# Twelve products for the last two up blocks of a delta-rule and hard-swish kernel, with their buffers given back

## The chip, the cores and the metric

One core of a Trainium2 chip runs the whole program. The metric is device time in microseconds (us), the median of several executions. The engines are TensorE (PE in the profile; its weight loads are PEld), VectorE (DVE), ScalarE (ACT), GpSimd (POOL) and SyncE (SP), which issues most DMAs here. Each engine works through its own queue in order, and semaphores make one wait for another. Every number of type float32 stays float32; in the profile a matmul of such numbers appears as two passes, each with its weight load.

## The reference

The first half is a delta-rule attention over 4 batches, 8 heads, 768 tokens and 48 channels; its output, as 3072 rows of 384, goes through an MLP with a hard-swish of 2048 channels.

```python
def _attn_ref(q, k, v, beta):
    B, H, S, D = q.shape                       # 4, 8, 768, 48
    k_n = k / (np.linalg.norm(k, axis=-1, keepdims=True) + 1e-06)
    state = np.zeros((B, H, D, D), dtype=np.float32)
    y = np.zeros_like(q)
    for t in range(S):
        kt, vt, bt = (k_n[:, :, t], v[:, :, t], beta[:, :, t, None])
        y[:, :, t] = np.einsum('bhd,bhde->bhe', q[:, :, t], state)
        v_old = np.einsum('bhde,bhd->bhe', state, kt)
        state = state + bt[:, :, :, None] * np.einsum('bhd,bhe->bhde', kt, vt - v_old)
    return y

def _moe_ref(x, w_in, w_out):                  # x 3072 x 384, w_in 384 x 2048, w_out 2048 x 384
    h = x @ w_in
    relu6 = np.clip(h + 3.0, 0.0, 6.0)
    g = h * relu6 / 6.0
    return g @ w_out
```

## The kernel before

**Tiles.** The 768 tokens are cut into N = 24 chunks of C = 32; a chunk t covers the four batches, 128 rows in all, one on each partition. Two chunks make a block of 256 rows for the MLP, so there are 12 blocks, 0 to 11.

**The chain.** For each chunk, `prep` (L492) scales the keys (`kb`, on GpSimd), builds a mask times beta (`mb`, L473, GpSimd), turns keys and queries on TensorE (`pt`) and copies them with ScalarE into a tile KQ (L521), multiplies them (`sc`) and lets VectorE make L and LB of the product (L545). `scaled` (L481) makes `bkb`, the keys times beta, on GpSimd. A triangular system is solved for each chunk: chunk 0 by `product` (L556), chunks 1 to 4 by `halves_of` and `join` (L653), with a scratch tile VY, and later groups of four by `inverse` (L733), some 60 VectorE instructions between two transpositions (L456, L460). `chain` (L774) then runs the recurrence over the chunks: `ks` (keys and queries times state, L793), R (VectorE, L806), `pz` (L814), Z (ScalarE, L901, into R's tile), `su` and the state's update (L912, L928), `py`, y (L830, L806, L849), and the transposition `yt` (L859), which is copied into the MLP's input xT (L863).

**The MLP.** `up` (L956) makes a block's hidden rows in 16 steps f of 128 channels. A step is three products over NKT = 3 slices of 128 input channels, each a matmul with 128 x 128 weights and 256 columns, added up in one of NPM = 4 PSUM banks (`ph`, L968). ScalarE's relu (L976) and VectorE's minimum and product (L979) make the hard-swish g; the bank is free when L979 has read it. `up_by_eleven` (L1032) is used in its place for blocks 10 and 11 (UF = 10, L993). There, two steps f and two halves of the columns are joined to a 2 x 2 problem in quarters for the first two slices, done with seven products for eight, and the third slice is added with four plain ones: eleven products of 128 columns in place of twelve. It needs sums of weights (`weight_sums`, L1007, GpSimd, during the down product of block 9) and of inputs (`token_sums`, L1023, VectorE, L1029), and puts g together from the first four products with ScalarE's copy (L1053), GpSimd's sums (L1005), VectorE's sums (L1069, L1070) and ScalarE's and VectorE's last steps (L1076, L1080, L1083). The first four products of a pair are issued by `begin(j)`, the other seven by `end(j)`.

The down product of block 0 and 1 is plain (`down`, L1122). From block 2 on `down_by_seven` (L1176) works with quarters again: A11 and A12 are g of f = 0 to 7 for the first and the second 128 rows, A21 and A22 those of f = 8 to 15. Seven products of 192 columns (`po`, L1196) of eight f each follow in the order 1, 4, 2, 5, 7, 6, 3, each in two halves of four f; VectorE makes sums in the place of A22, A21, A11 and A12 (L1182) between them, ScalarE copies results (L1203), and VectorE joins them (L1206) into `o`, which goes to DRAM (L1120).

**The order.** Nothing is reordered by a scheduler. Up to chunk 5 the order is the text ORDER, in which each word advances one generator by a step: `v` is one DMA of V, `q`, `k` and `w` those of queries, keys and weights. From chunk LS = 5 on, a loop of NU = 15 units per chunk advances the chain by a plan and takes one unit of the MLP (a step f, or half a down product) and two or three steps of the inverse in each. Block 9's up product runs beside chunk 20's chain, block 10's beside chunk 22's, and block 11's after the last chain has ended.

**Buffers.** `sums_in` (L116) is the memory of the weight sums. Until they are made it serves as spare room: two VY tiles (NVY = 2), every second mask `mb` of the early chunks, and the first of eight `bkb`. KQ has NKQ = 6 tiles, LB has 7, V has NVF = 2; R has one, which Z uses as well, so that R of chunk t waits for `py` and `su` of t - 1 (L882). `ring` and `needs` only assert at build time that the order allows a reuse; the waits themselves come from the tiles.

Of the kernel before, what the change touches and what calls it, by code (L numbers as in the profile page):

```python
# [38 lines left out]
k*2 v h4 i2*2 u rb i2 gb n9 i2 u i2 v i2 ru i2 gu i2 u ru i2*3 q gu i2 c n9 u k i2 u i2 u ru gu q  # L39
ru i2 gu i2 k n9 i2 u h4 y4 i2*2 n9 u y4 i2 q u*2 i2 u n9 ru i2*3 q k gu q*2 i2 n9 q i2*3 n9 u k  # L40
n9 q e i2*4 ru u gu y4 h4 e n9 u y4 k n9 k*2 i2 k*5 i2*2 k*3 ru k ru gu i2 u gu p9 u e i2 u i2*5 e
u i2*4
# [4 lines left out]
def kernel(  # L47
# [61 lines left out]
    def first(g):  # L109
# [3 lines left out]
    LA, LE, LS = 6, 4, G0 + GS  # L113
    NKB, NQB, NBKB, NLB, NKQ, NVY = 2, 4, 8, 7, 6, 2
    NPR = NFC // 2
    sums_in = persist.tile([P, 3, NPR, P], FP32, name="sums_in")  # L116
    spares = sums_in[:].rearrange("p n j c -> p (n j c)")
    vys = [spares[:, 4 * H * C * i : 4 * H * C * (i + 1)] for i in range(NVY)]
    mb_spare = spares[:, 8 * H * C : 10 * H * C]
    bkb_spare = spares[:, 10 * H * C : 10 * H * C + H * DP].rearrange("p (h w) -> p h w", w=DP)  # L120
    assert 10 * H * C + H * DP == 3 * NPR * P
    kbufs = [persist.tile([P, H, DP], FP32, name=f"kb{i}") for i in range(NKB)]
    qbufs = [persist.tile([P, H, DP], FP32, name=f"qb{i}") for i in range(NQB)]
    bkbufs = [bkb_spare] + [
        persist.tile([P, H, DP], FP32, name=f"bkb{i}") for i in range(1, NBKB)
    ]

    def bkb_of(t):
        return bkbufs[t if t < NBKB else 1 + (t - 1) % (NBKB - 1)]

# [46 lines left out]
    NVF = 2  # L177
# [284 lines left out]
    def mask(t):  # L462
        early = t < LS + LE
        if t > 1 or not early:
            needs(("L", t - (2 if early else 1)))
        if early and t % 2 == 0:
            mb = mb_spare.rearrange("p (e a j w) -> p e a j w", e=2, j=2, w=C)
        else:
            mb = work.tile([P, 2, NP, 2, C], FP32, name="mb", bufs=1)
        mbs[t] = mb  # L470
        needs("beta")
        for e in range(2):
            nc.gpsimd.tensor_tensor(  # L473
                out=mb[:, e],
                in0=beta_tok[:, t, e:H:2].unsqueeze(2).unsqueeze(3).to_broadcast([P, NP, 2, C]),
                in1=mask2[:].unsqueeze(1).to_broadcast([P, NP, 2, C]),
                op=ALU.mult,
            )
        yield

    def scaled(t):  # L481
        needs(("kb", t), *pad(t), *([("bkb", t - NKB)] if t >= NKB else []))
        if t >= NBKB:
            needs(("su", t - NBKB + 1))
        nc.gpsimd.tensor_tensor(
            out=bkb_of(t)[:, :, 0:D], in0=kbufs[t % NKB][:, :, 0:D],
            in1=beta_tok[:, t, 0:H].unsqueeze(2).to_broadcast([P, H, D]), op=ALU.mult,
        )
        past.add(("bkb", t))
        yield  # L490
# [65 lines left out]
    def product(t):  # L556
# [10 lines left out]
        ring("VY", NVY, ("x", t))  # L567
        VYTF = vys[t % NVY].rearrange("p (n w) -> p n w", w=H * C)
# [84 lines left out]
    def join(t):  # L653
# [7 lines left out]
        ring("VY", NVY, ("x", t))  # L661
        tiles = vys[t % NVY].rearrange("p (n h c) -> p n h c", n=4, c=C)
# [111 lines left out]
    def chain(t, whole=True):  # L774
# [8 lines left out]
        bkb = bkb_of(t)  # L783
# [96 lines left out]
        else:  # L880
            needs("parity")
            needs(("BZ", t - 1), ("su", t - 1))  # L882
# [17 lines left out]
        Zt = Rt if t > 0 else work.tile([P, DM], FP32, name="R", bufs=1)  # L900
# [21 lines left out]
        past.add(("su", t))  # L922
# [18 lines left out]
    mode = {"slow": False}  # L941
# [50 lines left out]

    UF = 10  # L993
    S1, S2, S4 = (sums_in[:, i] for i in range(3))

    def w_tiles(s, i):
        return w_in[:, s].rearrange("p (j i c) -> p j i c", i=2, c=P)[:, :, i]

    W11, W12, W21, W22 = w_tiles(0, 0), w_tiles(1, 0), w_tiles(0, 1), w_tiles(1, 1)
    W13, W23 = w_tiles(2, 0), w_tiles(2, 1)  # L1000
    T1x, T2x, T4x = (beta_tok[:, 8 * i : 8 * i + 8, 8:24] for i in range(3))
    assert H == 8 and N == 24

    def plus_minus(out, a, b, op):
        nc.gpsimd.tensor_tensor(out=out, in0=a, in1=b, op=op)  # L1005

    def weight_sums():  # L1007
        for j in range(0, NPR, 2):
            r = slice(j, j + 2)
            plus_minus(S1[:, r], W21[:, r], W22[:, r], ALU.add)  # L1010
            yield
            plus_minus(S2[:, r], S1[:, r], W11[:, r], ALU.subtract)
            yield
            plus_minus(S4[:, r], W12[:, r], S2[:, r], ALU.subtract)
            yield
            plus_minus(W21[:, r], W11[:, r], W21[:, r], ALU.subtract)
            yield

    def x_tiles(blk):
        x = xTs[blk]  # L1020
        return [x[:, s, i * P : i * P + P] for s in range(NKT) for i in range(CB)]

    def token_sums(blk):  # L1023
        needs(("seam", blk * CB), ("seam", blk * CB + 1), ("up", blk - 1))
        B11, B12, B21, B22, _, _ = (
            x.rearrange("p (a b) -> p a b", b=16) for x in x_tiles(blk)
        )
        for out, a, b in ((T1x, B12, B11), (T2x, B22, T1x), (B12, B22, B12), (T4x, B21, T2x)):
            nc.vector.tensor_tensor(out=out, in0=a, in1=b, op=ALU.subtract)  # L1029
        past.add(("sums", blk))  # L1030

    def up_by_eleven(blk):  # L1032
        needs(("sums", blk))
        mode["slow"] = True
        B11, T3x, B21, B22, B31, B32 = x_tiles(blk)
        phs, ready = {}, {}

        def mm(ph, n, w, x, start=False, stop=False):
            nc.tensor.matmul(  # L1039
                ph[:, n], lhsT=w, rhs=x, start=start, stop=stop, skip_group_check=True  # L1040
            )

        def begin(j):
            key = ("ph", blk, "by", j)
            ring("pm", NPM, key)
            ph = phs[j] = psM.tile([128, 4, P], FP32, name="ph", tag="pm")
            mm(ph, 0, W11[:, j], B11, start=True)
            mm(ph, 1, S1[:, j], T1x)
            mm(ph, 2, W21[:, j], T3x)
            mm(ph, 3, S2[:, j], T2x)  # L1050
            gs[blk, j] = mlp.tile([128, 2, TB], FP32, name="g", bufs=NFC // 2)
            gt = gs[blk, j][:].rearrange("p i (t c) -> p (i t) c", c=P)
            nc.scalar.activation(out=gt, in_=ph[:], func=ACTF.Copy)  # L1053
            plus_minus(gt[:, 1], gt[:, 1], gt[:, 2], ALU.add)
            plus_minus(gt[:, 2], gt[:, 0], gt[:, 1], ALU.add)
            plus_minus(gt[:, 0], gt[:, 0], gt[:, 3], ALU.add)

        def end(j):
            ph = phs.pop(j)
            mm(ph, 0, W12[:, j], B21)  # L1060
            mm(ph, 1, S4[:, j], B22)
            mm(ph, 2, W22[:, j], T4x)
            mm(ph, 0, W13[:, j], B31)
            mm(ph, 1, W13[:, j], B32)
            mm(ph, 2, W23[:, j], B31)
            mm(ph, 3, W23[:, j], B32, stop=True)
            g = gs[blk, j][:].rearrange("p i c -> p (i c)")
            gt = gs[blk, j][:].rearrange("p i (t c) -> p (i t) c", c=P)
            nc.vector.tensor_tensor(out=gt[:, 3], in0=ph[:, 3], in1=gt[:, 2], op=ALU.add)  # L1069
            nc.vector.tensor_tensor(  # L1070
                out=gt[:, 1:3], in0=ph[:, 1:3],
                in1=gt[:, 0].unsqueeze(1).to_broadcast([128, 2, P]), op=ALU.add,
            )

            def first():
                nc.scalar.activation(out=gt[:, 0], in_=ph[:, 0], func=ACTF.Copy)  # L1076
                read(("ph", blk, "by", j))
                ro = mlp.tile([128, CB, DM], FP32, name="o", bufs=1)
                r = ro[:].rearrange("p c m -> p (c m)")[:, 0 : 2 * TB]
                nc.scalar.activation(out=r, in_=g, func=ACTF.Relu, bias=half, scale=1.0 / 6.0)  # L1080

                def rest():
                    nc.vector.scalar_tensor_tensor(  # L1083
                        out=g, in0=r, scalar=1.0, in1=g, op0=ALU.min, op1=ALU.mult
                    )

                ready[j] = rest

            ready[j] = first
            if j == NPR - 1:  # L1090
                past.add(("up", blk))

        def go(j):
            if j in ready:
                ready.pop(j)()

        begin(0)
        yield
        begin(1)
        yield  # L1100
        for j in range(NPR):
            end(j)
            go(j - 1)
            if j + 2 < NPR:
                yield
                begin(j + 2)
                go(j)
                yield
            else:
                go(j)  # L1110
                if j == NPR - 1:
                    go(j)
                    mode["slow"] = False
                yield
# [378 lines left out]
```

## Time and profile before

| | |
|---|---|
| median of 3 runs | 687.84 us (685.55 to 689.42) |
| the profiled execution's own time | 685.55 us |
| its span, first to last instruction | 683.8 us |
| granted TensorE clock, mean over the span | 0.990 |
| instructions in the span | 25829 |
| up products by twelve, L968 (passes, busy, mean) | x1056, 227.4 us, 368 ns |
| of these with 256 columns | x864, 199.6 us, 382 ns |
| down products, L1196 | x1120, 112.1 + 86.7 us |
| GpSimd's sums of g, L1005 | x48, 21.8 us, 455 ns |

A line of the page's groups names line, engine, operation, tiles, shape and count, then busy time and the mean of one. The mean of a matmul pass is its time from start to its modelled end; passes overlap, so the time between starts is shorter than the mean. In a list in order of time, the columns are start in us, duration in us, engine, line, operation, tiles and count, and in brackets the idle time before it with what ended it.

### The profile page before, as it was taken

The numbers are of one execution on the slowest core, as the hardware profiler recorded it, in microseconds if no ns is written. First come the engines' busy times: TensorE is split into PE (matmuls) and PEld (weight loads), VectorE is DVE, ScalarE is ACT, GpSimd is POOL, SyncE is SP. The second block draws the span as 40 slices with busy tenths as digits, with TensorE's granted clock in tenths as the row PEclk, the third lists the DMA queues.
The fourth block names the chain that finished last, engine by engine and source line by source line (L and its number), as shares of the span: only waits on it lengthen the run. The fifth ranks groups of instructions, "written<-read, shape, count | busy, mean of one in ns | idle before, by whom it ended". The sixth has DMA issues, their size and how long they took to land.

```text
span 683.8 us, 25829 instructions
## 1 busy us (share of the span) xinstructions
PE 647.7 (95%) x11368; PEld 572.6 (84%) x11368; DVE 475.2 (69%) x1234; ACT 253.3 (37%) x503; POOL 118.3 (17%) x200
## 2 busy tenths in 40 slices
PE   2588989999999999999999999999999999999997
PEld 2468977776689989989988988978988989999997
DVE  5888867898556996746985746985546995457354
ACT  5986776423133133232133132132232132143250
POOL 6240232002311100100100101102000032040230
PEclk9997999999999999999999999999999999999999
DMA  7995435402040030041030030020020020100000
GB/s 182 246 215 132 99 88 130 80 4 45 23 86 14 3 72 2 3 89 19 2 71 2 3 71 2 2 61 2 3 47 2 3 48 2 28 11 2 25 1 23
DMA packets 88496, 33.23 MB, mean 49 GB/s; under 512 B 80160, under 2 KB 83232, under 8 KB 88384
## 3 DMA queue, kind: packets, MB, share of 16 engines
q1 hardware_dynamic: 88128, 31.29, 20.5%
q8 instruction: 89, 1.46, 0.9%
q10 hardware_dynamic: 256, 0.30, 0.2%
q14 instruction: 23, 0.19, 0.1%
HBM read 26.84 MB, written 4.72 MB: 46 GB/s over the span
## 4 chain that ended last, share of the span: by engine, by line
PE 78%; DVE 16%; issue 2%; ACT 2%; DMA 1%; SPq 0%; POOL 0%; DVEq 0%; ACTq 0%
PE ph L968 28%; PE po L1196 22%; PE ph L1039 6%; PE po L1131 4%; PE pt L513 3%; PE ks L793 3%; DVE g L1182 3%; PE py L814 3%; PE su L912 3%; PE pz L814 2%; DVE A L751 2%; DVE pr L746 2%; PE sc L534 2%; PE yt L859 1%; PE pi L671 1%
## 5 line engine op out<-in xcount | busy, mean ns | idle before, releaser
L968 PE MATMUL ph<-xT,w_in 128*128 128x256 f32 (+1 forms) x1056 | 227.4, 368 | 3.4 <-DVE g L979 2.8
L968 PEld LDWEIGHTS ph<-xT,w_in 128*128 128x128 f32 x1056 | 185.3, 194 | 27.7 <-DVE g L979 3.9
L976 ACT ACTIVATE g<-ph,halves 128x256 f32<-128x256 f32 (+1 forms) x176 | 79.1, 453 | 165.5 <-PE ph L968 163.4
L979 DVE SCALAR_TENSOR_TENSOR g<-g,ph 128x256 f32<-128x256 f32 (+1 forms) x176 | 68.1, 391 | 67.4 <-ACT g L976 67.2
L1196 PE MATMUL po<-w_out,g 128*128 128x192 f32 x640 | 112.1, 326 | 0.0
L1196 PEld LDWEIGHTS po<-w_out,g 128*128 128x128 f32 x640 | 104.7, 190 | 0.4
L1196 PE MATMUL po<-spare,g 128*128 128x192 f32 x480 | 86.7, 332 | 0.0
L1196 PEld LDWEIGHTS po<-spare,g 128*128 128x128 f32 x480 | 77.2, 190 | 1.8
L1182 DVE TENSOR_TENSOR g<-g 128x256 f32<-128x256 f32 x160 | 65.7, 459 | 3.3 <-PE po L1196 3.2
L473 POOL TENSOR_TENSOR mb<-beta_tok,mask 128x256 f32<-128x256 f32 x38 | 25.9, 702 | 236.8 <-DVE LB L545 236.8
L751 DVE TENSOR_TENSOR A<-A,pr 128x30 f32<-128x30 f32 (+9 forms) x150 | 53.7, 358 | 3.4
L746 DVE TENSOR_TENSOR pr<-A 128x30 f32<-128x30 f32 (+9 forms) x150 | 52.0, 347 | 3.1
L348 ACT ACTIVATE spare<-spare,places 128x768 uint16<-128x768 uint16 (+1 forms) x56 | 52.4, 940 | 2.9 <-DMA spare<-in_moe_w_in_dram 2.0
L1131 PE MATMUL po<-w_out,g 128*128 128x384 f32 x128 | 45.6, 493 | 0.0
L1203 ACT ACTIVATE o<-po 128x192 f32<-128x192 f32 x40 | 13.2, 330 | 82.4 <-PE po L1196 82.4
L521 ACT ACTIVATE KQ<-pt 128x512 f32<-128x512 f32 x48 | 28.1, 594 | 29.6 <-PE pt L513 29.2
L1039 PE MATMUL ph<-xT,w_in 128*128 128x128 f32 x224 | 34.2, 278 | 0.2
L497 POOL TENSOR_TENSOR kb<-kf,inv 128x384 f32<-128x384 f32 x24 | 22.3, 930 | 66.2 <-PE yt L859 35.6
L1131 PEld LDWEIGHTS po<-w_out,g 128*128 128x128 f32 x128 | 23.2, 190 | 12.4
L1005 POOL TENSOR_TENSOR g<-g 128x128 f32<-128x128 f32 x48 | 21.8, 455 | 67.8 <-ACT g L1053 65.3
L863 ACT ACTIVATE xT<-yt 128x384 f32<-128x384 f32 x24 | 11.7, 486 | 57.2 <-PE yt L859 57.2
L793 PEld LDWEIGHTS ks<-state,KQ 64*64 64x64 f32 x1472 | 24.8, 138 | 8.6 <-issue 7.7
(137 smaller groups left out, 779.7 us busy)
## 6 DMA issues: line engine op xcount, KB each, us to landing
kf<-in_k_dram SPq DMA_DIRECT2D x96, 48.0 KB, 2.7
qb<-in_q_dram SPq DMA_DIRECT2D x96, 48.0 KB, 2.9
vf<-in_v_dram SPq DMA_DIRECT2D x96, 48.0 KB, 2.1
out_dram<-o SPq DMA_DIRECT2D x92, 48.0 KB, 1.6
spare<-in_moe_w_in_dram SPq DMA_DIRECT2D x4, 768.0 KB, 7.6
w_out<-in_moe_w_in_dram SPq DMA_DIRECT2D x4, 768.0 KB, 7.1
w_out<-in_moe_w_out_dram SPq DMA_DIRECT2D x4, 768.0 KB, 6.6
spare<-in_moe_w_out_dram SPq DMA_DIRECT2D x4, 768.0 KB, 4.8
```

Of the source, the lines that this page charges most:

```text
L348: nc.scalar.activation(out=z, in_=z if n else d.bitcast(I16)[:, :, :, 3], func=func, bias=places[:, n : n + 1], scale=scale,)
L746: nc.vector.tensor_tensor(out=pv, in0=A[:, j + 1 :, j].unsqueeze(2).to_broadcast([n, w, j]), in1=A[:, j, 0:j].unsqueeze(1).to_broadcast([n ...
L751: nc.vector.tensor_tensor(out=A[:, j + 1 :, 0:j], in0=A[:, j + 1 :, 0:j], in1=pv, op=ALU.subtract)
L793: nc.tensor.matmul(ph[y][c, e, D * p : D * p + D], lhsT=KQ[r, p * B // 2 + b // 2, 2 * y : 2 * y + 2, :].rearrange("k y c -> k (y c)"), rh ...
L814: nc.tensor.matmul(ps[rows(place(b)), D * h : D * h + D], lhsT=m(h)[rows(b)], rhs=z[rows(b), D * h : D * h + D], start=True, stop=True, sk ...
L968: nc.tensor.matmul(ph[:, cols], lhsT=w_in[:, s, f * 128 : (f + 1) * 128], rhs=xT[:, s, cols], start=(s == 0), stop=(s == NKT - 1),)
L976: nc.scalar.activation(out=g, in_=ph, func=ACTF.Relu, bias=half, scale=1.0 / 6.0)
L979: nc.vector.scalar_tensor_tensor(out=g, in0=g, scalar=1.0, in1=ph, op0=ALU.min, op1=ALU.mult)
L1039: nc.tensor.matmul(ph[:, n], lhsT=w, rhs=x, start=start, stop=stop, skip_group_check=True)
L1131: nc.tensor.matmul(pos[c][:], lhsT=gs[blk, f // 2][:, f % 2, c * P : (c + 1) * P], rhs=w_out[:, f, :], start=(f == 0), stop=(f == NFC - 1),)
L1182: nc.vector.tensor_tensor(out=A(f, *out), in0=A(f, *a), in1=A(f, *b), op=op)
L1196: nc.tensor.matmul(ps[n][:], lhsT=A(f - f % 2, *a)[:, f % 2], rhs=b[:, f], start=(f == 0), stop=(f == HF - 1),)
```

## The change

Blocks 10 and 11 use `up`, like the others; `up_by_eleven`, `weight_sums`, `token_sums` and the slower step of the inverse that went with them are gone. `sums_in` is gone, and what had been in its room has tiles of its own or joins another ring: VY takes tiles of KQ's ring, which has seven for six; `mb` has two tiles throughout; `bkb` has eight tiles used in turn; LB has eight for seven; V three for two; Z has its own tile. `down_by_seven` begins with products 4, 2, 1 in place of 1, 4, 2, in every block, and the first sums stand two half products later against product 4. ORDER has four more steps of V loads near its end. The squares of the norms (L398) are ScalarE's in both kernels.

```diff
+k*2 v h4 i2*2 u rb i2 gb n9 i2 u i2 v i2 ru i2 gu i2 u ru i2*3 v q gu i2 c n9 u k i2 u i2 u ru gu
+q ru i2 gu i2 k n9 v i2 u h4 y4 i2 v*2 i2 n9 u y4 i2 q u*2 i2 u n9 ru i2*3 q k gu q*2 i2 n9 q i2*3
...
-    LA, LE, LS = 6, 4, G0 + GS
-    NKB, NQB, NBKB, NLB, NKQ, NVY = 2, 4, 8, 7, 6, 2
-    NPR = NFC // 2
-    sums_in = persist.tile([P, 3, NPR, P], FP32, name="sums_in")
...
+    NKB, NQB, NBKB, NLB, NKQ = 2, 4, 8, 8, 7
...
-    bkbufs = [bkb_spare] + [
-        persist.tile([P, H, DP], FP32, name=f"bkb{i}") for i in range(1, NBKB)
-    ]
...
+    bkbufs = [persist.tile([P, H, DP], FP32, name=f"bkb{i}") for i in range(NBKB)]
...
-    NVF = 2
+    NVF = 3
...
-        if early and t % 2 == 0:
-            mb = mb_spare.rearrange("p (e a j w) -> p e a j w", e=2, j=2, w=C)
-        else:
-            mb = work.tile([P, 2, NP, 2, C], FP32, name="mb", bufs=1)
-        mbs[t] = mb
+        mb = mbs[t] = work.tile([P, 2, NP, 2, C], FP32, name="mb")
...
-        ring("VY", NVY, ("x", t))
-        tiles = vys[t % NVY].rearrange("p (n h c) -> p n h c", n=4, c=C)
+        ring("KQ", NKQ, ("x", t))
+        tiles = work.tile([P, 4, H, C], FP32, name="VY", tag="KQ", bufs=NKQ)
...
-            needs(("BZ", t - 1), ("su", t - 1))
...
-        Zt = Rt if t > 0 else work.tile([P, DM], FP32, name="R", bufs=1)
+        Zt = work.tile([P, DM], FP32, name="Z", bufs=1)
...
-    def weight_sums():
...
-    def token_sums(blk):
...
-    def up_by_eleven(blk):
...
         settle()
+        product(4, A22, T4, 0)
+        yield
+        product(4, A22, T4, 1)
+        copy(C21, 4, -1.0)
+        yield
+        product(2, A12, B21, 0)
+        yield
+        product(2, A12, B21, 1)
+        copy(C11, 2)
+        sums(ALU.add, A22, A21, A22, lo)
+        yield
         product(1, A11, B11, 0)
+        sums(ALU.add, A22, A21, A22, hi)
         yield
         product(1, A11, B11, 1)
         copy(u, 1)
-        yield
-        product(4, A22, T4, 0)
-        yield
-        product(4, A22, T4, 1)
-        copy(C21, 4, -1.0)
-        sums(ALU.add, A22, A21, A22, lo)
-        yield
-        product(2, A12, B21, 0)
-        sums(ALU.add, A22, A21, A22, hi)
-        yield
-        product(2, A12, B21, 1)
-        copy(C11, 2)
         sums(ALU.subtract, A21, A11, A21, lo)
         yield
         product(5, A22, T1, 0)
...
-            sums = weight_sums() if blk == UF - 1 else iter(())
...
-                for n, _ in enumerate((up_by_eleven if blk + 1 >= UF else up)(blk + 1)):
+                for n, _ in enumerate(up(blk + 1)):
...
-                12: lambda: token_sums(t // CB) if t % CB and t // CB >= UF else None,
...
-                take(fill, 1 if mode["slow"] else 2 + (u % 3 == 0))
+                take(fill, 2 + (u % 3 == 0))
```

## The prediction

> **What bounds the kernel now.** I read the busy shares first, then the waits of TensorE, then the stretches of the last two blocks, then single instructions in order of time.
>
> ```profile
> PE 647.7 (95%) x11368; PEld 572.6 (84%) x11368; DVE 475.2 (69%) x1234; ACT 253.3 (37%) x503; POOL 118.3 (17%) x200
> ...
> PE 78%; DVE 16%; issue 2%; ACT 2%; DMA 1%; SPq 0%; POOL 0%; DVEq 0%; ACTq 0%
> ```
>
> TensorE is busy for 95% of the span and holds 78% of the chain that ended last. The next view lists whom TensorE waited for: line, releaser, total us, times, longest.
>
> ```profile
> PE pt L513 <- POOL kb L497: 8.2, 1, 8.2
> PE ph L968 <- DVE g L979: 2.8, 3, 1.2
> PE ph L1039 <- DVE beta_tok L1029: 1.0, 2, 0.5
> ```
>
> Most of its 36 us of idle time lies in the first 100 us. After 171 us the list in order of time has only the three waits on L979 (2.8 us), one of 0.2, and the two on L1029. So from there a change counts by the TensorE time it adds or takes. The stretches of the last blocks (start and end in us, length, then busy us of PE, PEld, DVE, ACT, POOL with counts, granted clock, DMA):
>
> ```profile
> 546.08:571.24 25.16, 25.16 (x356) 21.55 (x356) 21.45 (x55) 8.45 (x18) 9.38 (x13) 1.00 0.16 34
> ...
> 593.88:619.09 25.21, 24.62 (x438) 23.70 (x436) 13.23 (x34) 11.73 (x24) 10.86 (x24) 1.00 0.11 26
> 619.09:640.92 21.83, 21.83 (x310) 20.95 (x309) 12.34 (x34) 4.82 (x11) 0.00 (x0) 1.00 0.01 2
> 640.92:661.69 20.77, 20.21 (x178) 19.86 (x177) 9.80 (x25) 10.40 (x21) 10.90 (x24) 1.00 0.08 20
> ```
>
> The first is the up product of block 9 by twelve products; the second and fourth are those of blocks 10 and 11 by eleven; the third is the down product of block 10. Block 9 and block 10 carry the same chain work between their products (ks, pz, su, py, yt), block 11 none. The reader sees it at once: 25.21 us by eleven against 25.16 by twelve, with TensorE never idle in the latter.
>
> **The change part by part.** *Eleven becomes twelve in blocks 10 and 11.* In instructions, a product is two passes. By twelve a block is 16 x 3 x 2 = 96 passes of 256 columns, by eleven 8 x 11 x 2 = 176 of 128. The price of a pass comes from the time between starts:
>
> ```profile
> 503.33 5.45 PE L968 MATMUL ph<-xT,w_in 128*128 128x256 f32 x24
> 508.71 0.88 PE L814 MATMUL pz<-R,X 32*32 32x48 f32 x64
> ...
> 594.79 0.46 PE L1039 MATMUL ph<-beta_tok,sums_in 128*128 128x128 f32 x2 [0.52 <-DVE beta_tok L1029]
> ...
> 654.32 1.28 PE L1039 MATMUL ph<-xT,w_in 128*128 128x128 f32 x10
> 655.43 0.39 PE L1039 MATMUL ph<-beta_tok,sums_in 128*128 128x128 f32 x2
> ```
>
> 24 passes take 508.71 - 503.33 = 5.38, so 0.224 each; ten short ones take 1.11, so 0.111 each. Half the columns cost half. Eleven therefore needs 176 x 0.111 = 19.5 and twelve 96 x 0.224 = 21.5: a nominal loss of 2.0 a block if eleven goes. But eleven does not get its 2.0. Its second product needs T1x, which the vector engine makes at L1029, and after this wait and the restarts block 11 takes 20.77, 1.2 over its 19.5. In block 10 the chain work takes 3.85 between starts (ks 1.07, pz 0.82, su and py 1.63, yt 0.33), so 25.21 is 1.8 over 19.5 + 3.85. What eleven gains it loses by its start.
>
> After the change block 10 is what block 9 is now: 25.16, or -0.05. Block 11 is block 9 less the chain, 25.16 - 3.85 = 21.31, or 96 passes at 0.224, 21.5; I take 21.4, or +0.65. Sum: +0.6 us. The two ends are +0.5 and +0.75.
>
> A rule speaks against this: the Trainium skill, "TensorE: Matmul & The Clock Gate", section "Back-to-back issue gap", gives a sustained 81 ns for a matmul of 128 columns and 131 for 512, so short ones cost far more per column. Read off a straight line at 98 for 256, its twelve would take 96 x 98 against 176 x 81, a third less, and the change would gain about 6.7 us a block, 13 in all. The rows above have 0.111 against 0.224 and show no such surcharge; the rows decide.
>
> *What the other engines lose and gain in these blocks.* Gone: GpSimd's 16 weight sums (11.8 us) and 48 sums of g at 455 ns (21.8); ScalarE's L1053, L1076 and L1080 (9.6, 4.4, 11.6); VectorE's L1029, L1069, L1070 and L1083 (2.4, 4.7, 6.8, 10.9). Added: 32 L976 at 473 ns on ScalarE (15.1) and 32 L979 at 417 ns on VectorE (13.3). Each unit of three products lasts 6 x 0.224 = 1.34 us, so 0.47 and 0.42 lie beneath TensorE, as in block 9, where VectorE has 21.45 of 25.16 and still stops nothing. Blocks 10 and 11 have no inverse to fill VectorE besides. Cost 0; uncovered, a late L979 would hold one of four ph banks, as it does three times now for 0.8 to 1.2 us.
>
> *The order in every down product: 4, 2, 1 for 1, 4, 2.* TensorE's matmuls stay the same. New is that the first product reads A22, g of f = 8 to 15, right after these were made, where A11 (f = 0 to 7) stood. From block 8's start:
>
> ```profile
> 523.44 2.76 PE L1196 MATMUL po<-w_out,g 128*128 128x192 f32 x16
> ...
> 524.14 0.42 DVE L979 SCALAR_TENSOR_TENSOR g<-g,ph 128x256 f32<-128x256 f32 x1 [0.26 <-ACT g L976]
> ...
> 526.13 1.15 PE L793 MATMUL ks<-state,KQ 64*64 64x48 f32 x64
> ```
>
> Sixteen passes take 2.69, so f = 15, the eighth pair, is wanted 7 x 0.336 = 2.35 after the start, at 525.79. Its g is done at 524.14 + 0.42 = 524.56, 1.12 after the start: 1.2 us to spare, as in the blocks before it (1.13 after the start in blocks 2 and 3, 1.12 in block 4). Behind a late g everything on TensorE would queue, ks first, then R, pz, Z and the state. I take 0. On the other side VectorE's sums for A22 no longer follow the product they overwrite:
>
> ```profile
> DVE g L1182 <- PE po L1196: 3.2, 13, 0.6
> POOL sums_in L678 <- DVE sums_in L689: 30.0, 2, 17.7
> SPq L185 <- DVE R L806: 16.3, 4, 7.0
> ```
>
> These 3.2 us come free, but the next thing on VectorE at that place is y (L806), which waits for ScalarE's y, still behind a copy that ends with the same half product; the time is waited there. I take 0, with a gain of at most the 2.8 us of TensorE's waits on L979.
>
> *Buffers.* VY moves into the KQ ring (seven for six, VY included), mb gets two buffers throughout, LB eight, V three, bkb eight of its own, and Z no longer shares R's tile. The order of instructions to block 2 stays but for the four V loads made earlier, and as many fewer later. This frees GpSimd's memset at L678 (30.0 us idle) and the V loads on SP's queue (16.3 us), behind which K, Q and weight loads stand. The built program adds waits too: KQ copies on ScalarE after GpSimd's memset of the slot, with relus queued behind them, and the last memset after the first ks, in place of L689. But TensorE waits for GpSimd once, at the start, and for K, Q or V never; ScalarE's only waits for a K load are at 4.8 and 6.7 us, before all this. Freed or held, they have cover. Value 0. From above the gain is TensorE's idle time on other engines in 60 to 110 us: 0.48 + 1.05 + 0.55 + 0.44 = 2.5 us (before 64.66, 66.44, 87.14 and 106.92 in its list in order of time). From below, an added wait costs at most as much again.
>
> So the profiled span goes from 683.8 to 684.4, its device time from 685.55 to 686.15. The median of the runs shown is 2.3 above that execution, 687.84; with +0.6 I forecast **688.4**.
>
> **Rivals.** *The freed waits were the real price (faster).* For it: 16.3 us on SP's queue, 30.0 on GpSimd's, 3.2 on VectorE's, at a time when TensorE is not full. Against it: TensorE names none of them. All of it: -2.5 - 2.8 + 0.6 = -4.7, so 683.1. It also covers a dearer short pass than the starts show. Chance 0.12.
>
> *A22 first makes TensorE wait at each of ten down products (slower).* For it: VectorE is behind in three stretches, and a transposition (L460, 1.97 us) can come between. Against it: the 1.2 us to spare. From there on each further us is paid in full: one such transposition in front of the last g is 1.97 - 1.2 = 0.8, ten times 8, with 0.6 gives 696.4; at half the blocks, 692.4. Chance 0.09.
>
> *The start goes otherwise (mostly slower).* In windows of 5 us the granted clock from 50 to 55 us is 0.50, from 65 to 70 0.69, from 95 to 100 0.73; shifting TensorE's gaps shifts these. One more 5 us stretch at half clock with TensorE full costs 2.5, two cost 5: 691 to 693.4. Against it: the gaps' causes are not touched. Chance 0.09.
>
> *Eleven's own value, 4 us for two blocks if its start were free,* as the diff would suggest: 691.8. Only if the waits of L1029 came back elsewhere in after. Chance 0.05.
>
> **How the numbers follow.** 0.65 is left for the forecast, whose own range is 686.5 to 690.5: 0.6 with the spread of the runs shown, 685.55 to 689.42, about its middle. A measurement of this kernel tells 0.5%, 3.4 us, from no change. The four rivals give faster 0.11, slower 0.17; the rest, 0.72, within. The range reaches 684.0 to 692.0.
>
> **What would show it.** In the profile after: block 10's up stretch 25.2 and block 11's 21.4 us with TensorE never idle; 1056 + 2 x 96 = 1248 passes on the up line, L968 now; no wait of TensorE for the g of the last f at a down product; the three waits for g after blocks 2, 4 and 6 still 2 to 3 us in all; GpSimd's 30 us at the memset gone, TensorE's gaps from 50 to 110 us as they are. Wrong it would be if the stretch before 214 us changes by over 2 us, or a new wait stands in front of product 4.

## The result and the profile after

The changed kernel takes 691.99 us (median of 20 runs, 686.76 to 694.71), the kernel before in the same runs 688.40 (683.82 to 692.34). The ratio is 1.0045, with a 95% interval from 1.0024 to 1.0066: slower, by less than the 0.5% that a measurement of this kernel tells from no change. A second measurement (12 runs, below) gives 1.0009 (0.9981 to 1.0036). Over all 32 runs the mean is 691.18 us. The kernel before was timed again beside every group of kernels here, 119 runs in all, with a mean of 689.01: 2.2 us less, uncertain by 0.9.

The profiled execution after has a span of 690.5 us, 6.7 more than that of before. Its page, the busy shares and the chain that ended last:

```profile
PE 649.9 (94%) x11208; PEld 569.7 (83%) x11208; DVE 467.4 (68%) x1210; ACT 244.4 (35%) x487; POOL 84.9 (12%) x136
...
PE 76%; DVE 17%; issue 3%; ACT 2%; DMA 1%; SPq 0%; POOL 0%; DVEq 0%; ACTq 0%; POOLq 0%
```

GpSimd (POOL) has 33 us less to do, TensorE about as much as before, and the chain leans a little more on VectorE. The waits (engine, line, releaser: total us, times, longest) that answer to those shown of before; the up product's line is now L942, the relu's product L953, the sums' L1033, the V load's L171:

```profile
PE pt L490 <- POOL kb L474: 8.5, 1, 8.5
PE ph L942 <- DVE g L953: 3.6, 5, 1.7
...
DVE g L1033 <- PE po L1047: 0.4, 2, 0.2
...
SPq L171 <- DVE R L783: 5.5, 3, 3.5
```

GpSimd's 30.0 us at the memset are gone from the list, of VectorE's 3.2 behind the first product 0.4 are left, and of SP's 16.3 there are 5.5. But TensorE waits for g five times where it waited three times. The stretches of the last blocks, in the columns of the prediction's table (start and end, length, busy us of PE, PEld, DVE, ACT, POOL, granted clock, DMA):

```profile
600.20:625.36 25.16, 25.16 (x357) 21.56 (x356) 10.02 (x25) 8.44 (x18) 0.00 (x0) 1.00 0.07 18
625.36:647.19 21.83, 21.83 (x309) 20.95 (x307) 10.53 (x30) 3.57 (x9) 0.00 (x0) 1.00 0.01 2
647.19:667.91 20.72, 20.72 (x98) 18.24 (x97) 6.68 (x16) 7.10 (x15) 0.00 (x0) 1.00 0.07 20
```

Blocks 10 and 11 by twelve products take 25.16 and 20.72 us, by eleven they took 25.21 and 20.77: the removal of eleven is worth 0.1 us. Nothing is lost there. The loss is in the front, as the stretch up to block 2's down product is called from here on. Block 2's down product begins at 222.01 for 213.93, 8.08 us later; from there to the end it is 468.49 us for 469.87, 1.38 *shorter*. One place in the front stands out, where the same steps take longer than before (in order of time, with start and duration; VectorE and GpSimd together, from the changed kernel):

```profile
55.16 1.25 POOL L452 TENSOR_TENSOR mb<-beta_tok,mask 128x256 f32<-128x256 f32 x2
55.28 0.63 DVE L694 TENSOR_TENSOR pr<-A 128x52 f32<-128x52 f32 x1
55.94 0.54 DVE L699 TENSOR_TENSOR A<-A,pr 128x52 f32<-128x52 f32 x1
56.37 0.82 POOL L462 TENSOR_TENSOR bkb<-kb,beta_tok 128x384 f32<-128x384 f32 x1
...
56.51 0.77 DVE L694 TENSOR_TENSOR pr<-A 128x72 f32<-128x72 f32 x1
...
57.30 0.82 POOL L462 TENSOR_TENSOR bkb<-kb,beta_tok 128x384 f32<-128x384 f32 x1
57.32 0.90 DVE L699 TENSOR_TENSOR A<-A,pr 128x72 f32<-128x72 f32 x1
```

and the same steps of VectorE in the kernel before, where GpSimd starts nothing after 48.27 until 66.35 us:

```profile
53.64 0.21 DVE L717 TENSOR_TENSOR pr<-A 128x52 f32<-128x52 f32 x1
53.88 0.22 DVE L722 TENSOR_TENSOR A<-A,pr 128x52 f32<-128x52 f32 x1
54.13 0.23 DVE L717 TENSOR_TENSOR pr<-A 128x72 f32<-128x72 f32 x1
54.40 0.23 DVE L722 TENSOR_TENSOR A<-A,pr 128x72 f32<-128x72 f32 x1
```

Four steps of the triangular inverse (`halves_of`) take 0.63 + 0.54 + 0.77 + 0.90 = 2.84 us for 0.89. That is 1.95 us, beside mb and bkb, which GpSimd now makes here because nothing holds it at the memset. VectorE is late with g behind these steps, and TensorE has two waits that this execution of before did not have (the bracket holds the wait and its releaser):

```profile
60.86 2.31 PE L942 MATMUL ph<-xT,w_in 128*128 128x128 f32 x18 [1.73 <-DVE g L953]
63.48 2.72 PE L942 MATMUL ph<-xT,w_in 128*128 128x128 f32 x22 [0.31 <-DVE g L953]
```

The waits alone are no proof of the cause. In the traces below, the seven in which GpSimd is free have 1.09 to 3.37 us of them at this place, but three of the seven in which it is held have some as well: 0.24 us in e6, 1.01 in e11 and 2.08 in e3, with short steps.

### The profile page after: what moved, and what is told of

It is laid out like the page before. It is cut to its first block, busy times and chain, and to the rows that moved or that the text cites. A ratio compares the mean times of both kernels' runs of the same rounds, so it can differ in the third digit from the quotient of the medians.

```text
span 690.5 us, 25323 instructions
## 1 busy us (share of the span) xinstructions
PE 649.9 (94%) x11208; PEld 569.7 (83%) x11208; DVE 467.4 (68%) x1210; ACT 244.4 (35%) x487; POOL 84.9 (12%) x136
## 3 DMA queue, kind: packets, MB, share of 16 engines
q8 instruction: 88, 1.44, 0.9%
## 4 chain that ended last, share of the span: by engine, by line
PE 76%; DVE 17%; issue 3%; ACT 2%; DMA 1%; SPq 0%; POOL 0%; DVEq 0%; ACTq 0%; POOLq 0%
PE ph L942 33%; PE po L1047 21%; PE po L982 4%; PE ks L770 3%; PE pt L490 3%; PE py L791 3%; DVE pr L723 3%; DVE A L728 3%; PE pz L791 2%; PE su L888 2%; DVE g L1033 2%; PE sc L511 2%; PE yt L836 1%; DVE o L1057 1%; ACT spare L334 1%
## 5 line engine op out<-in xcount | busy, mean ns | idle before, releaser
L942 PE MATMUL ph<-xT,w_in 128*128 128x256 f32 (+1 forms) x1248 | 271.7, 371 | 5.1 <-DVE g L953 3.6
L942 PEld LDWEIGHTS ph<-xT,w_in 128*128 128x128 f32 x1248 | 222.6, 194 | 34.5 <-DVE g L953 4.7
L950 ACT ACTIVATE g<-ph,halves 128x256 f32<-128x256 f32 (+1 forms) x208 | 94.3, 456 | 200.7 <-PE ph L942 200.6
L953 DVE SCALAR_TENSOR_TENSOR g<-g,ph 128x256 f32<-128x256 f32 (+1 forms) x208 | 81.6, 396 | 100.4 <-ACT g L950 100.1
L1047 PE MATMUL po<-spare,g 128*128 128x192 f32 x480 | 84.8, 330 | 0.0
L1033 DVE TENSOR_TENSOR g<-g 128x256 f32<-128x256 f32 x160 | 64.1, 454 | 0.5 <-PE po L1047 0.4
L452 POOL TENSOR_TENSOR mb<-beta_tok,mask 128x256 f32<-128x256 f32 x48 | 34.2, 733 | 90.6 <-DVE LB L522 90.6
L783 DVE SCALAR_TENSOR_TENSOR y<-ks,parity,y 128x192 f32<-128x192 f32 x46 | 17.1, 413 | 20.1 <-ACT y L807 20.0
L770 PE MATMUL ks<-state,KQ 64*64 64x48 f32 x1472 | 28.0, 225 | 2.4 <-issue 2.4
```

Of the source, the lines that this page charges most:

```text
L452: nc.gpsimd.tensor_tensor(out=mb[:, e], in0=beta_tok[:, t, e:H:2].unsqueeze(2).unsqueeze(3).to_broadcast([P, NP, 2, C]), in1=mask2[:].unsq ...
L770: nc.tensor.matmul(ph[y][c, e, D * p : D * p + D], lhsT=KQ[r, p * B // 2 + b // 2, 2 * y : 2 * y + 2, :].rearrange("k y c -> k (y c)"), rh ...
L942: nc.tensor.matmul(ph[:, cols], lhsT=w_in[:, s, f * 128 : (f + 1) * 128], rhs=xT[:, s, cols], start=(s == 0), stop=(s == NKT - 1),)
L950: nc.scalar.activation(out=g, in_=ph, func=ACTF.Relu, bias=half, scale=1.0 / 6.0)
L953: nc.vector.scalar_tensor_tensor(out=g, in0=g, scalar=1.0, in1=ph, op0=ALU.min, op1=ALU.mult)
L1033: nc.vector.tensor_tensor(out=A(f, *out), in0=A(f, *a), in1=A(f, *b), op=op)
```

## The experiments

The theory (A): buffers freed GpSimd, and its work now runs beside short VectorE steps on the path, which it slows. Rivals: the V loads made earlier (B), the chance of one execution's front (C), and for the 1.38 us gained later, the order of the products or Z's own tile (D). e1 to e12 are the labels of the runs; each was timed 12 times, e10 6 times. "Measured" is the ratio to the kernel before in the same measurement, with its 95% interval. What was expected before a run calls the chunks tokens.

**GpSimd held again (e1).** The changed kernel, in `join`:

```
+        held = work.tile([P, HC], FP32, name="held", bufs=2)
+        nc.gpsimd.tensor_copy(out=held[:], in_=corner[:])
         nc.gpsimd.memset(S[:, :, 0:HC], 0.0)
...
-            out=S[:, :, HC:C], in0=ps[:], in1=corner[:]...
+            out=S[:, :, HC:C], in0=ps[:], in1=held[:]...
```

> The changed kernel, but GpSimd waits again in front of the memset of join(3) and join(4): it first copies the 16 columns of corner into one of two small tiles, which VectorE's sum in join(t - 2) reads. VY stays in the KQ ring. Theory A (freed, GpSimd multiplies mb and bkb beside VectorE's small triangular steps at 52 to 60 us, and these, on which TensorE waits, take 0.5 to 0.9 us for 0.2): the steps go back to 0.2 us, block 2's down product starts 2 to 5 us earlier than in the changed kernel (217 to 220 for 222.0), time 0.996 to 1.000 of before. Theory B (the V loads made earlier delay what the front needs) and theory C (the front's 8 us are chance of that one execution): start and time as in the changed kernel, 1.004 to 1.005 for B; for C a start anywhere.

Measured: 1.0002 (0.9979 to 1.0025). GpSimd waits 30.6 us at the copy, mb comes at 68.52 us, and the steps are short again:

```profile
56.01 0.20 DVE L696 TENSOR_TENSOR pr<-A 128x52 f32<-128x52 f32 x1
56.24 0.21 DVE L701 TENSOR_TENSOR A<-A,pr 128x52 f32<-128x52 f32 x1
56.49 0.23 DVE L696 TENSOR_TENSOR pr<-A 128x72 f32<-128x72 f32 x1
56.76 0.23 DVE L701 TENSOR_TENSOR A<-A,pr 128x72 f32<-128x72 f32 x1
```

Block 2's down product starts at 219.55 us, 2.46 earlier; that says little, since the changed kernel's second execution (e8) starts it at 219.80. In the means of all runs e1 is at 688.81, the changed kernel at 691.18: 2.4 us, uncertain by 1.3. The changed kernel, e2, e4 and e5 below all leave GpSimd free; their 68 runs have a mean of 691.01, 2.2 over e1, uncertain by 1.2. A holds here, and B does not explain it, for the V loads are as in the changed kernel.

**The old order of the products (e2).** Products 1, 4, 2 and VectorE's sums where they stood before:

```
+        product(1, A11, B11, 0) ... copy(u, 1)
         product(4, A22, T4, 0)  ... copy(C21, 4, -1.0)
         product(2, A12, B21, 0) ... copy(C11, 2)
-        product(1, A11, B11, 0) ... copy(u, 1)
```

> The changed kernel, with the down products in the order before, 1, 4, 2, and VectorE's sums where they stood. If the order is what shortened TensorE's three waits for g after blocks 2, 4 and 6 (2.84 to 1.59 us), they come back to 2.8 and the time is 1.2 us over the changed kernel, 1.006 of before; the stretch in front of block 2's down product stays at 222. If they were shortened by something else (where VectorE stands after the front), 1.0045 and waits of about 1.6.

Measured: 1.0032 (1.0014 to 1.0050). The three waits for g after blocks 2, 4 and 6 are 0.17, 1.07 and 0.46, 1.70 in all for 1.59; from block 2's down product to the end it takes 468.59 for 468.49. So the order is worth 0.1 us, and the gain is not its doing.

**Twelve products alone (e3).** The kernel before with `UF = 13` for 10.

> The kernel before, with all blocks by twelve products (UF = 13) and nothing else changed: buffers, order and front as before. By the prediction's sum 0.6 us more, 1.001; by the trace of the changed kernel (blocks 10 and 11 in 25.16 and 20.72 us for 25.21 and 20.77) 0.1 us less, 1.000. The front and the three waits for g stay as in the kernel before. If twelve products were the cause of the slower time, 1.0045.

Measured: 0.9991 (0.9970 to 1.0013). From block 2's down product to the end 469.73 for 469.87, as the changed kernel's blocks 10 and 11 said. Its front, with the very instructions of the kernel before, is 3.9 us longer in this execution (217.87 for 213.93): much of the 8.08 can be chance, and rival C has a part.

**Two V buffers again (e4).** `NVF = 2` for 3 and the old order of the loads, in the changed kernel.

> The changed kernel with two V buffers for three and the order of the V loads as before. Theory B (earlier V loads share the queue with what the front waits for): the front loses its 8 us or a good part of it, 0.996 to 1.000 of before. Theory A: nothing, 1.0045, and block 2's down product starts at about 222.

Measured: 1.0032 (1.0007 to 1.0056), the four slowed steps again 0.63, 0.54, 0.77 and 0.90, and block 2's down product at 225.66 us, not earlier. B falls.

**Z in R's tile again (e5).** In `chain`:

```
+            needs(("BZ", t - 1))
...
-        Zt = work.tile([P, DM], FP32, name="Z", bufs=1)
+        Zt = Rt if t > 0 else work.tile([P, DM], FP32, name="R", bufs=1)
```

> The changed kernel, with Z written into R's tile again. Theory D (the own tile for Z shortened TensorE's three waits for g, since VectorE need not wait before it writes R): the three waits after blocks 2, 4 and 6 are 2.8 us in all again for 1.6, and from block 2's down product to the end takes 469.7 us for 468.5; the time 1 us over the changed kernel. Rival (mb, LB or bkb did it): 468.5 stays, and the time as the changed kernel's.

Measured: 1.0018 (0.9993 to 1.0042); the three waits 1.77 us, the rest of the span 468.19. D falls with both its halves.

**GpSimd held, and mb's second buffer taken back (e6).** e1, and in `mask`:

```
+        early = t < G0 + GS + 4
+        if t > 1 or not early:
+            needs(("L", t - (2 if early else 1)))
+        name = "mb2" if early and t % 2 == 0 else "mb"
+        mb = mbs[t] = work.tile([P, 2, NP, 2, C], FP32, name=name, bufs=1)
```

> e1_gpsimd_held, and mb's two buffers used as in the kernel before: two for the early tokens, one alone afterwards. Theory A, second place (two buffers let GpSimd make one mb and one bkb more at 167 us, beside VectorE's steps of 128x84 and 128x58, which take 0.54 and 0.73 for 0.24 and 0.22): those steps go back, block 2's down product starts 1.1 us earlier against the start of the front (219.6 to 218.5 if nothing else differs), time 0.998 to 0.999 of before. Rival (the second place costs nothing, since VectorE has room there): the steps go back, but the start and the time stay, 1.000.

Measured: 0.9979 (0.9958 to 1.0001). Both sides of mb's second buffer show. The stretch from the inverse's step at 158.89 us to block 2's down product is 57.82 us; the changed kernel's, from 163.10, is 58.91. And the rest of the span is 469.49, the three waits 0.72 + 0.83 + 0.83 = 2.38. So the second buffer loses 1.1 us in front and gains 1.1 behind.

**The kernel before with GpSimd freed (e7).** Two memsets that only write zeros over zeros are left out:

```
+        if t < 3:
             nc.gpsimd.memset(S[:, :, 0:HC], 0.0)
```

> The kernel before, without the memsets of join(3) and join(4), whose zeros still stand in the reused buffer from join(1) and join(2). GpSimd does two instructions less and no longer waits 30 us. Theory A: its mb and bkb then run at 51 to 58 us beside VectorE's small steps, four of these take 2.84 us for 0.89, and the kernel gets slower by 2 to 3 us: 1.003 to 1.004. Rival (the freed GpSimd is harmless, and the copy of corner in e1 helped in another way, or the result of e1 was chance): 1.000 or less.

Measured: 0.9996 (0.9974 to 1.0017), where A had 1.003 to 1.004. VectorE's steps are slowed here too: at 54.42 and 55.34 us two of 128x28 take 0.89 and 0.92 for 0.20 and 0.21, and the triangle, the steps of `halves_of` from the first to the last, takes 10.38 us for 8.99. The time does not show these 1.4 us: the interval ends at 1.0017, 1.2 us over the kernel before. In the means e7 is 0.4 us over it, uncertain by 1.2. So this run, the only one that frees GpSimd and changes nothing else, excludes the 2 to 3 us expected and leaves the smaller price open.

**The changed kernel again (e8).** No edit.

> The changed kernel once more, for a second execution of its front and a closer ratio: 1.0045 by the first measurement; the four slowed steps of VectorE at 55 to 58 us again 0.63, 0.54, 0.77 and 0.90, from block 2's down product to the end 468.5. Theory A expects these to be the same in every execution, and the rest of the front's 8.1 us to vary: a start of block 2's down product between 218 and 224.

Measured: 1.0009 (0.9981 to 1.0036); the four steps as before to a hundredth, block 2's down product at 219.80 for 222.01, the rest 468.30.

**Both holds (e9).** e1, with mb's two buffers in turn, but chunk 10's mb in the buffer of chunk 9's:

```
+        name = "mb2" if (t + (t > 9)) % 2 else "mb"
+        mb = mbs[t] = work.tile([P, 2, NP, 2, C], FP32, name=name, bufs=1)
```

> e1_gpsimd_held, with mb's two buffers in turn throughout, but token 10's mask in the same buffer as token 9's, so that GpSimd is held once more there (at 167 us in the changed kernel). By e5 and e6 the two buffers for mb shorten the three waits for g, and their price is the three slowed steps at 167 us. Theory: both gains together, from block 2's down product to the end 468.5 as in the changed kernel, no slowed 128x84 and 128x58 steps before it, time 1.1 us under e1, 0.997 to 0.999 of before. Rival (the steps at 167 us are covered): as e1, 1.000.

Measured: 1.0002 (0.9976 to 1.0028), where 0.997 to 0.999 was expected. In its profile both gains stand together, 57.82 in front of block 2's down product and 468.48 behind it; in the time 1.1 us is too little to be seen, and the interval holds theory and rival alike.

**The suspected cost made larger (e10).** In the changed kernel, bkb of chunks 3 and 4 three times over:

```
+        for _ in range(3 if t in (3, 4) else 1):
             nc.gpsimd.tensor_tensor(out=bkbufs[t % NBKB]...
```

> The changed kernel with the multiplication of bkb for tokens 3 and 4 issued three times each (the same values are written again): 4 x 0.82 = 3.3 us more of GpSimd's work at 58 to 61 us, and nobody waits for it before 100 us. Theory A: more of VectorE's small triangular steps take 0.5 to 0.9 us for 0.23 to 0.28, some 2 to 3 us in all, and TensorE's wait for g grows by as much: 0.3 to 0.4% over the changed kernel, whose 32 runs lie 0.33% over the kernel before, so 1.006 to 1.008. Rival (slowed steps are covered by other work; the freed GpSimd costs in another way): the steps slow, the time stays at 1.002 to 1.004.

Measured: 1.0104 (1.0078 to 1.0130), more than the 1.006 to 1.008 expected, with a mean of 694.84 us, 3.7 over the changed kernel, uncertain by 1.7. Its own VectorE and GpSimd:

```profile
57.53 2.64 POOL L463 TENSOR_TENSOR bkb<-kb,beta_tok 128x384 f32<-128x384 f32 x3
57.68 0.77 DVE L695 TENSOR_TENSOR pr<-A 128x72 f32<-128x72 f32 x1
58.48 0.87 DVE L700 TENSOR_TENSOR A<-A,pr 128x72 f32<-128x72 f32 x1
59.39 0.89 DVE L695 TENSOR_TENSOR pr<-A 128x88 f32<-128x88 f32 x1
...
60.27 2.64 POOL L463 TENSOR_TENSOR bkb<-kb,beta_tok 128x384 f32<-128x384 f32 x3
60.31 0.90 DVE L700 TENSOR_TENSOR A<-A,pr 128x88 f32<-128x88 f32 x1
61.24 0.89 DVE L695 TENSOR_TENSOR pr<-A 128x100 f32<-128x100 f32 x1
62.16 0.87 DVE L700 TENSOR_TENSOR A<-A,pr 128x100 f32<-128x100 f32 x1
63.07 0.27 DVE L695 TENSOR_TENSOR pr<-A 128x108 f32<-128x108 f32 x1
```

A bkb comes every 2.64 / 3 = 0.88 us (a single one takes 0.83), and as long as they last VectorE gets one step done for each of them, the first in 0.77, the others in 0.87 to 0.90 us; the first step after the last of them takes 0.27 again. The triangle takes 14.35 us for 10.94, 3.4 more, near what the time lost. TensorE first reads one of these bkb at 129.93 us (su of chunk 3). It is the clearest of the runs: GpSimd's work, which nobody waits for, is paid through VectorE, and as far as the time can tell in full.

**mb's second buffer alone (e11).** e3 with `early = True` in `mask` for all chunks:

> e3_twelve_alone (the kernel before, twelve products throughout) with mb's two buffers in turn for all tokens, GpSimd held at the memsets as before. If mb's second buffer is what shortened the three waits for g and what slowed the steps at 167 us: waits 1.6 us for 2.8, from block 2's down product to the end 468.5 for 469.7, three slowed steps of 128x84 and 128x58 in front of it, and a time like e3's, 0.999, since 1.2 us gained and 1.1 lost cancel. If neither comes, VY in the KQ ring or the other buffers are in it.

Measured: 0.9985 (0.9962 to 1.0008). 58.93 us in front of block 2's down product for 57.84, and 467.74 behind it for 469.73; of the three waits the first is gone, the others are 0.71 and 1.07.

**The same, held at chunk 10 (e12).** e11, but mb for chunk 10 in chunk 9's buffer, and in turn from there.

> e11, with token 10's mask in token 9's buffer, as in e9. Theory: the gain without the price, 468.5 and no slowed steps at 167 us: 1.2 us under e3, 0.997 to 0.998 of before, and faster than the kernel before and the changed one. Rival: as e3, 0.999.

Measured: 0.9981 (0.9950 to 1.0011); 57.83 and 467.81. e11 and e12 together (24 runs, mean 687.42) lie 1.85 us under the kernel before beside them (29 runs, 689.27), uncertain by 1.2, and 3.8 under the changed kernel. They lie only 0.6 under e3 (twelve products alone, 688.03), uncertain by 1.3, and e12 lies 0.1 under e11: what mb's second buffer and its hold add shows in the traces, not in the time.

The second place where GpSimd slows VectorE, in the changed kernel (mb and bkb of one more chunk):

```profile
166.63 1.22 POOL L452 TENSOR_TENSOR mb<-beta_tok,mask 128x256 f32<-128x256 f32 x2
166.83 0.54 DVE L723 TENSOR_TENSOR pr<-A 128x84 f32<-128x84 f32 x1
167.41 0.54 DVE L728 TENSOR_TENSOR A<-A,pr 128x84 f32<-128x84 f32 x1
167.81 0.83 POOL L462 TENSOR_TENSOR bkb<-kb,beta_tok 128x384 f32<-128x384 f32 x1
167.98 0.73 DVE L723 TENSOR_TENSOR pr<-A 128x58 f32<-128x58 f32 x1
```

and the same steps in e12, where nothing runs on GpSimd beside them:

```profile
160.89 0.25 DVE L745 TENSOR_TENSOR pr<-A 128x84 f32<-128x84 f32 x1
161.17 0.24 DVE L750 TENSOR_TENSOR A<-A,pr 128x84 f32<-128x84 f32 x1
161.45 0.22 DVE L745 TENSOR_TENSOR pr<-A 128x58 f32<-128x58 f32 x1
```

Three steps with 0.29 + 0.30 + 0.51 = 1.10 us more, and the stretch to block 2's down product is some 1.1 longer in every kernel that has them: here nothing covers them. In each of these kernels TensorE waits 1.44 us for ScalarE's y in front of `sc` some 11 us later, in the others 0.62 to 0.64.

The profiled executions side by side, worked out from starts in the traces: up to VectorE's first 128x28 step, from there to the end of its last (the triangle), on to the inverse's 128x150 subtraction, on to block 2's down product, and the rest of the span; the clock is the mean granted from 0 to block 2's down product.

| kernel | to 128x28 | triangle | middle | to block 2's down | rest | clock |
|---|---|---|---|---|---|---|
| before | 52.42 | 8.99 | 94.68 | 57.84 | 469.87 | 0.97 |
| e3 twelve alone | 54.85 | 9.23 | 95.95 | 57.84 | 469.73 | 0.96 |
| e7 before, freed | 54.42 | 10.38 | 99.00 | 57.83 | 469.77 | 0.95 |
| e11 mb two | 52.06 | 8.98 | 96.49 | 58.93 | 467.74 | 0.96 |
| e12 mb two, held | 52.76 | 9.44 | 94.96 | 57.83 | 467.81 | 0.97 |
| changed | 54.06 | 10.94 | 98.10 | 58.91 | 468.49 | 0.95 |
| e8 changed again | 54.87 | 10.94 | 95.05 | 58.94 | 468.30 | 0.98 |
| e2 old order | 54.91 | 10.95 | 95.32 | 58.93 | 468.59 | 0.97 |
| e4 two V | 54.68 | 10.93 | 101.12 | 58.93 | 468.44 | 0.92 |
| e5 Z in R | 52.55 | 11.87 | 98.65 | 58.94 | 468.19 | 0.94 |
| e1 held | 54.79 | 8.98 | 96.85 | 58.93 | 468.35 | 0.96 |
| e6 held, mb single | 52.71 | 8.99 | 97.19 | 57.82 | 469.49 | 0.97 |
| e9 both holds | 51.68 | 8.98 | 97.34 | 57.82 | 468.48 | 0.98 |
| e10 bkb thrice | 55.22 | 14.35 | 98.66 | 58.94 | 468.53 | 0.93 |

The fourth column has two values only, with mb's second buffer unheld or not; the rest depends on mb's second buffer alone to within 0.9 us. The triangle takes 8.98 to 9.44 us where GpSimd is held, 10.38 to 11.87 where it is free, and 14.35 in e10 (e5's four slowed steps are those of the changed kernel; its 0.9 us more are not). The first column and the middle differ by some 3 and 6 us among kernels whose instructions there are nearly the same (98.10 and 95.05 for the changed kernel itself).

## Why the prediction was right, and where not

**The time.** 688.4 was forecast, and a change of under 0.5% was called the likeliest case. The ratio is 1.0045, so that case holds, though 691.99 lies over its own range (to 690.5) and at the very end of the whole one (684.0 to 692.0). That it is still inside is luck in part: the upper end was there for the spread and for rivals other than what happened, and the term that moved the time stood at 0.

**Eleven becomes twelve: +0.6.** Block 10 was put at 25.16 and takes 25.16. Block 11 was put at 21.4 and takes 20.72: 96 passes at 0.216, where the prediction took 0.224 from a stretch of 24. The term of +0.65 is -0.05. The other way to it, block 9 less the chain, was off by 0.6: block 10 less block 11 is now 4.44 us, where the chain was put at 3.85. e3 gives the whole as -0.14 in the profile. "What eleven gains it loses by its start" was right.

**The other engines in these blocks: 0.** Right: TensorE is busy for every us of the three stretches.

**The order 4, 2, 1: 0.** Right. Product 4 waits for no g, and e2 finds 0.1 us. That VectorE's 3.2 us would come free and be waited for ScalarE's y is in line with the waits: 3.2 went to 0.4, and VectorE's wait for y from 15.3 to 20.0. TensorE's waits for g did shrink, from 2.84 to 1.59, but through mb's second buffer (e6, e11), not through these sums. How the second buffer does it is only half followed: with one buffer, mb, bkb and kb run in a row behind VectorE's LB (229.66 to 232.88 us in e6), with two they stand apart (221.68, 228.71 and 233.93 in e9), and the next g of VectorE lies 0.55 us nearer to the start of block 2's down product.

**The buffers: 0.** This is the step that failed. "Freed or held, they have cover" asked who waits for GpSimd and found TensorE once, at the start, which is true. It did not ask beside what the freed work would run. The held GpSimd kept mb and bkb away from VectorE's short steps; freed, it costs 1.95 us in the triangle and 1.10 at 167 us. The prediction's bounds for the buffers, 2.5 us either way, came from TensorE's waits and added waits, and this price is in neither. With the 1.38 gained in the rest, 1.95 + 1.07 - 1.38 = 1.6 us, and 2.2, uncertain by 0.9, were measured in the time. That the freed GpSimd is what costs rests on e10, on e1 and on the held kernels as a group: e1, e6 and e9 have a mean of 688.54 in 36 runs, the changed kernel, e2, e4 and e5 691.01 in 68, 2.5 more, uncertain by 0.8 (e6 and e9 lack the slow steps at 167 us as well). e7 speaks neither for it nor, at its size of 1.4 us, clearly against it.

The Trainium skill has the rule: "SBUF — State Buffer", section "Who interferes with whom", says that a VectorE instruction with two inputs in SBUF contends with a GpSimd instruction that reads SBUF. The same page, section "Summary: rules for kernel authors", says that of the two the second to issue is blocked until the first is done. e10's rows agree: steps of 0.87 to 0.90, each begun just behind a bkb of 0.83 and ended just after it. It was the rule to weigh against this change, and the prediction weighed another.

**"The stretch before 214 us changes by over 2 us"** was named as what would prove the steps wrong, and it does: 8.08. By the table 1.64 come up to the triangle, 1.95 in it, 3.42 in the middle and 1.07 after. The second and the fourth are the change's; the first and the third vary as much between executions of like kernels, and e8 has 0.37 in the middle. Whether a freed GpSimd costs something there too stays open: the middle is 98.0 us on average in the seven executions where GpSimd is free and 96.2 in the seven where it is held, but the two sets overlap. Of the other signs, the 1248 passes came and GpSimd's wait went, but the three waits for g are 1.59 us, not 2 to 3, and TensorE's gaps in the front did not stay as they were.

**The rivals.** "Freed waits the real price" had the right place and the wrong sign. A22 first never made TensorE wait. "Eleven's own value" names 691.8, next to the measured 691.99, but by chance: e3 and the stretches show that nothing was lost in blocks 10 and 11. "The start goes otherwise" (691 to 693.4) came nearest, with another mechanism: not the clock's stretches alone, but VectorE beside GpSimd.

## What to carry to other kernels

When a buffer frees an engine from a wait, look not only at who waits for that engine, but at what runs on the others at the time its work moves to: GpSimd's elementwise work was not free here where VectorE had short two-input steps on the path. A wait can be a schedule worth keeping; where the buffer is wanted, the wait can be put back at the one place (e12, whose trace has the gain without the price). And where one kernel's front differs by 3 us and more from execution to execution, compare stretch by stretch over several profiles before a difference is given to the change.

## What the runs showed of the hardware

A 128x28 to 128x100 f32 tensor_tensor of VectorE, both inputs in SBUF, takes 0.18 to 0.27 us alone and mostly 0.87 to 0.92 (0.73 and 0.77 where it began later) beside a 128x384 f32 multiplication of GpSimd of 0.82 to 0.83; it takes 0.54 to 0.63 beside one of 128x256 of about 0.62. In the rows shown GpSimd's instruction began first and is not slowed: bkb takes 0.82 us in the changed kernel beside these steps. Where VectorE began first, GpSimd is the one that is late: in the kernel before, a bkb at 89.74 us takes 1.54, begun behind a two-input step of VectorE (L381, 128x768) that runs from 89.17 to 90.60. So the price on VectorE is counted here in GpSimd's instructions, one VectorE step for each, whatever the step's size.
